# Induced attention and a leaky feed-forward in one program: attention products in common TensorE clusters, longer assumed landings

## The chip, the cores and the metric

The program runs on one core of a Trainium2 chip. Its engines are TensorE (matrix products into the eight PSUM banks), VectorE (DVE in the rows), ScalarE (ACT), GpSimd (POOL) and SyncE (SP), which issues the DMA transfers. Each engine takes its instructions in the order in which the program has them, and waits for semaphores of the others. The metric is device time in microseconds (us): 1604.66 us median of three runs before the change (1601.34 to 1604.69).

## The reference

```
def mab(q, kv):                       # one attention, 32 keys or queries "inducing"
    s = scale * (q @ kv.T);  s = s - s.max(-1)
    a = exp(s);  a /= a.sum(-1) + 1e-09
    return a @ kv
h   = mab(inducing, x)                # per batch: 32 x 128, over 12480 rows
y   = mab(x, h)                       # per batch: 12480 x 128
out = leaky(y @ w_in) @ w_out         # 49920 rows, 128 -> 2048 -> 128, slope 0.01
```

All is float32: `x` is 4 x 12480 x 128, `inducing` 32 x 128, `w_in` 128 x 2048, `w_out` 2048 x 128.

## The kernel before

*Algebra.* The second attention's weights for a row are 32 numbers, so `y @ w_in` is these weights times `h @ w_in`, a 32-row matrix per batch. Leaky ReLU is split into a ReLU part and a linear part; the linear part needs only `h @ (w_in @ w_out)`. Each float32 product is made of three products of rounded parts (high x high, high x low, low x high), which run in the faster float32r form; tiles called `hi` and `lo` are those parts.

*Tiles.* A batch has six groups of 2048 rows and one of 192 (number `RG` in the code). A group is four tiles of 512 columns; the 192-row groups of two batches share one tile, the pair tile, whose place is `PAIR_AT`. For each tile there are 16 blocks of the feed-forward width. A block has three first products (`A4` with `hwhi`, `hwlo`), a ReLU, a split into `ghi` and `glo`, and then second products with `w_hi` and `w_lo`, three in each of four row groups. All these products are row-tiled: 32 rows of the array each, four at once (`quarter`, line 988). The split of a block has two forms: near (ScalarE makes `ghi` from the bank, line 975, VectorE makes `glo`, line 978) and far (ScalarE copies the ReLU to `g`, GpSimd makes both parts, lines 1216 and 1218).

*Attention work.* Per batch and group there is a score product of the first attention (line 372, with `indT`), a small product that spreads the maxima (406), a value product (`xr` rows with the weights, 535), and later a score product of the second attention (372, with `hT`). At the end of a batch come a sum (605), a transposition of h (624), and the expansion of h through the weights (752, 768). These use the array in other tilings than line 988. The second attention's softmax goes through VectorE, GpSimd and ScalarE into a tile `aT`; `stack` (line 842 on) casts it into `both` (high part on ScalarE at line 856, low part on GpSimd at 863), and SyncE copies it (878) into the row-tiled form `A4`, of which there are three buffers. `both` has one buffer, `xr` nine.

*What sets the order.* From the third tile to the last but one a planner in the kernel, run when the program is built, writes out the order. It keeps a clock for each engine, assumes a time for each operation (`RELU`, `LOW`, `QUARTER` and so on) and for a transfer's landing (`LANDED`), and takes what can start soonest. Attention work stands in lanes (generators): stacking, stores, seconds (second scores), values, middles (maxima), scores. A lane that needs TensorE asks for it with the time from which it could run. `clustered` decides when such asks are served between the row-tiled products: when one has waited 9 us (`OLD`), when two stand there and one has waited 3 us (`PAIRED`), or when TensorE would be idle for 0.3 us (`IDLE`); up to three at once (`TOGETHER`). First products run up to ten blocks (`GB`) ahead of the second ones. `relu` takes the far form only where GpSimd would be done before the block's turn comes:

```
far = max(clock[POOL], start + RELU) + backlog(POOL) + FAR_HIGH + FAR_LOW
wanted = now[0] + (i - turn_of[0]) * SLOT - EARLY
if far_open[0] < 2 and left <= start and far <= wanted:
```

The first scores of batch b + 1 begin with the first tile of batch b (`begin`); values of a batch follow group by group (`first_values`), where the loads of the next group's `xr` are asked behind the value product.

Of the kernel before, what the change touches and what calls it, by code (L numbers as in the profile page):

```python
# [19 lines left out]
def induced_attention_then_leaky_ffn(  # L20
# [66 lines left out]
    XR = 9  # L87
# [6 lines left out]
    LANDED = 2300.0  # L94
# [360 lines left out]
    def first_scores(b):  # L455
# [15 lines left out]
        for g in [RG, *range(RG)]:  # L471
            _, J, K = GROUPS[g]
            w = 32 * K
            if g == RG:
# [30 lines left out]
            at = on_array("c", 875.0 if g != RG else 120.0, at, taken[0])  # L505
            if quads[0]:
# [14 lines left out]
    middles = []  # L521
# [48 lines left out]
    def first_values(b):  # L570
# [11 lines left out]
        for g in [RG, *range(RG)]:  # L582
# [7 lines left out]
            hp, at = multiplied(b, g, ay, at)  # L590
            yield from new(DVE, at)
# [3 lines left out]
            if g == RG - 1:  # L595
                yield from new(PE)
# [3 lines left out]

    def sums(b):

        pz = aux_ps("z_ps")
        same = e128.rearrange("p j m -> p (j m)")
        nc.tensor.matmul(pz[:, :1], same, sums_of.pop(b), start=True, stop=True)
        at = on_array("f", 64.0, taken[0])
        rz = sb.tile([P, 1], F32, tag="rz", name="rz")
        nc.vector.tensor_scalar_add(rz, pz[:, :1], 1e-9)
        nc.vector.reciprocal(rz, rz)
        done(pz, spent(DVE, 330.0, at))  # L610
        return rz

    def normalise(b, hacc, rz):
# [17 lines left out]
        hw[b] = [hT, None, None, False]  # L631
        landed[b, "h"] = at
# [109 lines left out]
    def expand_weights(b):  # L742

        hT = hw[b][0]
        hi = sb.tile([P, TOK + P], F32R, tag="hwhi", name="hwhi", bufs=2)
        lo = sb.tile([P, TOK + P], F32R, tag="hwlo", name="hwlo", bufs=2)
        if b:
            yield from new(PE, landed.get((b, "h"), 0.0))
# [7 lines left out]
        at = on_array("c", 875.0, landed.get((b, "h"), 0.0), taken[0])  # L756
# [4 lines left out]
        yield from old(HEAVY)  # L761

    def expand_linear(b):
        hT, hi, lo, _ = hw[b]
        if b:
            yield from new(PE, landed.get((b, "h"), 0.0))
        pw = aux_ps("m2_ps")
        nc.tensor.matmul(pw[:, :P], hT, w12, start=True, stop=True)
        at = on_array("f", 220.0, landed.get((b, "h"), 0.0), taken[0])
# [4 lines left out]
        yield from old()  # L774


    def second(b, g, eng=None):
        eng = eng or nc.gpsimd
        yield from until(lambda: g == RG or sum(q != RG for _, q in aT) < 4)
# [9 lines left out]
        del xT[b, g]  # L789
        ring.discard((b, g))  # L790
# [51 lines left out]
    def stack(tiles_, eng=None):  # L842
# [26 lines left out]
        for t, parts in tiles_:  # L869
            yield from until(lambda: len(A4) < A4_BUFS)  # L870
            a4 = sb.tile([P, 2, TOK], F32R, tag="A4", name="A4", bufs=A4_BUFS)
            to = 0
            for b, g, js in parts:
                w, o = 32 * GROUPS[g][2], at[b, g]
                for j in js:
                    yield from new(SP, when)
                    for r in range(4):
# [4 lines left out]
                        landed["A", t] = landed["both"] = spent(SP, 640.0, when) + LANDED  # L882
# [6 lines left out]
    def quick(t):  # L889
# [13 lines left out]
        if not qys:  # L903
            qys.append(sb.tile([P, QUICK, 4, M], F32, tag="both", name="qy", bufs=1))
# [34 lines left out]
    PAIR_AT = 4  # L939
# [145 lines left out]
    def after_h(b):  # L1085
        yield from first_values(b)
        yield from expand_weights(b)
        yield from expand_linear(b)
# [13 lines left out]
    with tc.manual_schedule():  # L1102
# [25 lines left out]
        seconds = [second(0, 0, nc.vector)] + [second(0, g) for g in [1, 2, RG, 3, 4, 5]]  # L1128
# [383 lines left out]
```

## Time and profile before

| | |
|---|---|
| three runs | 1601.34, 1604.66, 1604.69 us |
| profiled execution | 1606.44 us, span of the core's instructions 1604.7 us |
| mean granted TensorE clock | 0.986 |
| instructions | 60005 |

The profile comes from one execution. A row of the timeline has the start in us from the span's start, the duration, the engine, the line of the kernel, the operation, its tiles (out<-in) and how many were merged into the row; in brackets the idle time before it and who ended it. PE is TensorE, PEld its weight loads, SPq and ACTq are an engine's queue. The windows view with one line counts the instructions of that line that start in a stretch. The chain of waits is followed back from the last instruction, at each step to what released it. In the orders no time stands; they list the instructions of an engine as the program has them.

### The profile page before, as it was taken

The page shows a single profiled execution, that of the slowest core. Times are in us where ns is not written, and L with a number is a line of the kernel's source. Part 1 is how long each engine was busy: PE and PEld are TensorE (multiplying, and loading weights), DVE is VectorE, ACT ScalarE, POOL GpSimd, SP SyncE. Part 2 cuts the span into 40 slices and gives each one's busy share as a digit, 9 for nine tenths or more (in the row PEclk, how much of TensorE's full clock was granted, in tenths as well). Part 3 has the DMA queues.
Part 4 walks back from the last instruction along what each step waited for, and adds up shares of the span by engine and source line. Part 5 has one row for each costly group of instructions (what it writes and reads, how often), then busy time and mean ns, then how long its engine had stood idle before and what let it go on. Part 6 is the DMA issues. An engine that isn't in the chain of part 4 may idle for free.

```text
span 1604.7 us, 60005 instructions
## 1 busy us (share of the span) xinstructions
PE 1565.6 (98%) x25047; PEld 1360.7 (85%) x25047; DVE 1084.6 (68%) x1914; ACT 1080.4 (67%) x1957; POOL 1179.3 (73%) x1227
## 2 busy tenths in 40 slices
PE   7989999999999999999999999999999999999998
PEld 5658878899997876889999877789898899999996
DVE  6667886665666867666666876566666677666665
ACT  6446657777775655667777566677777777777774
POOL 2028716999998255699999458999999957778773
PEclk9899999999999999999999999999999999999999
DMA  7155653223254557323234667233233233232231
GB/s 266 16 115 98 126 140 74 50 56 62 35 109 70 101 103 151 82 55 61 48 62 93 109 125 159 60 64 58 46 70 58 37 67 63 55 65 53 57 61 21
DMA packets 400704, 128.49 MB, mean 80 GB/s; under 512 B 373136, under 2 KB 375600, under 8 KB 400432
## 3 DMA queue, kind: packets, MB, share of 16 engines
q1 hardware_dynamic: 399328, 124.50, 38.7%
q8 instruction: 197, 3.23, 0.8%
q14 instruction: 75, 0.61, 0.1%
q10 hardware_dynamic: 1104, 0.15, 0.1%
HBM read 48.94 MB, written 25.56 MB: 46 GB/s over the span
## 4 chain that ended last, share of the span: by engine, by line
PE 89%; SPq 4%; DMA 4%; DVE 2%; issue 1%; ACT 1%; POOL 0%; ACTq 0%; DVEq 0%; POOLq 0%
PE bank L988 83%; PE bank L372 2%; DMA xr<-in_x_dram 2%; SPq L878 2%; SPq L357 1%; PE bank L1018 1%; PE bank L535 1%; DVE glo L978 1%; DMA raw<-in_moe_w_in_dram 1%; SPq L346 0%; DMA A<-both 0%; POOL glo L1218 0%; ACT ghi L975 0%; PE bank L406 0%; DMA out_dram<-osb 0%
## 5 line engine op out<-in xcount | busy, mean ns | idle before, releaser
L988 PE MATMUL bank<-ghi,w_hi 32*128 32x512 f32 (+1 forms) x6080 | 1221.3, 393 | 4.8 <-ACT ghi L975 4.8
L988 PE MATMUL bank<-ghi,w_lo 32*128 32x512 f32 (+1 forms) x6080 | 1214.6, 392 | 0.0
L988 PE MATMUL bank<-glo,w_hi 32*128 32x512 f32 (+1 forms) x6080 | 1213.7, 392 | 0.0
L988 PE MATMUL bank<-A,hwhi 32*128 32x512 f32 (+1 forms) x3394 | 1051.6, 392 | 9.1 <-ACT g L975 3.6
L978 DVE SCALAR_TENSOR_TENSOR glo<-bank,ghi 128x512 fp32r<-128x512 f32 (+1 forms) x1052 | 697.3, 682 | 362.9 <-ACT ghi L975 345.3
L988 PEld LDWEIGHTS bank<-ghi,w_hi 32*128 32x128 f32 x6080 | 775.4, 184 | 42.9 <-ACT ghi L975 6.0
L988 PEld LDWEIGHTS bank<-glo,w_hi 32*128 32x128 f32 x6080 | 770.0, 184 | 35.2 <-issue 9.8
L988 PEld LDWEIGHTS bank<-ghi,w_lo 32*128 32x128 f32 x6080 | 773.4, 184 | 31.0 <-issue 5.8
L975 ACT ACTIVATE ghi<-bank 128x512 fp32r<-128x512 f32 (+1 forms) x1052 | 611.5, 598 | 217.4 <-PE bank L988 187.6
L1218 POOL TENSOR_TENSOR glo<-g,ghi 128x512 fp32r<-128x512 f32 (+1 forms) x516 | 668.1, 1295 | 41.3
L988 PE MATMUL bank<-A,hwlo 32*128 32x512 f32 (+1 forms) x1697 | 621.6, 390 | 0.0
L988 PEld LDWEIGHTS bank<-A,hwhi 32*128 32x128 f32 x3394 | 569.1, 184 | 38.1 <-DVE glo L978 7.3
L975 ACT ACTIVATE g<-bank 128x512 f32<-128x512 f32 (+1 forms) x516 | 308.6, 598 | 210.2 <-PE bank L988 174.3
L1216 POOL CAST ghi<-g 128x512 fp32r<-128x512 f32 (+1 forms) x516 | 316.4, 613 | 135.6 <-ACT g L975 96.0
L988 PEld LDWEIGHTS bank<-A,hwlo 32*128 32x128 f32 x1697 | 302.5, 184 | 6.2 <-issue 1.4
L1261 POOL TENSOR_TENSOR part<-part 128x512 f32<-128x512 f32 (+1 forms) x95 | 123.0, 1295 | 96.3 <-DVE part L1250 93.3
L1250 DVE TENSOR_TENSOR part<-bank,part 128x512 f32<-128x512 f32 (+1 forms) x190 | 129.8, 685 | 64.2 <-PE bank L988 42.8
L1244 ACT COPY part<-bank 128x512 f32<-128x512 f32 (+1 forms) x190 | 110.4, 583 | 18.1 <-PE bank L988 14.9
L1037 DVE STREAM_TRANSPOSE osb<-part 128x512 f32<-128x512 f32 (+1 forms) x95 | 66.6, 701 | 11.2 <-POOL part L1261 10.5
L826 POOL TENSOR_TENSOR y<-y,sm 128x512 f32<-128x512 f32 (+1 forms) x27 | 25.4, 941 | 32.0 <-DVE sm L822 17.2
L495 DVE STREAM_TRANSPOSE xT<-xc 128x512 f32<-128x512 f32 x72 | 47.4, 689 | 1.3 <-DMA xc<-in_x_dram 1.3
L863 POOL TENSOR_TENSOR both<-aT,both 128x512 fp32r<-128x512 f32 x24 | 31.1, 1296 | 20.9 <-DMA xr<-in_x_dram 12.5
(120 smaller groups left out, 632.5 us busy)
## 6 DMA issues: line engine op xcount, KB each, us to landing
A<-both SPq DMA_DIRECT2D x376, 128.0 KB, 2.4
xr<-in_x_dram SPq DMA_DIRECT2D x96, 256.0 KB, 4.6
out_dram<-osb SPq DMA_DIRECT2D x382, 64.0 KB, 2.2
xc<-in_x_dram SPq DMA_DIRECT2D x288, 64.0 KB, 2.9
raw<-in_moe_w_in_dram SPq DMA_DIRECT2D x4, 512.0 KB, 6.6
raw<-in_moe_w_out_dram SPq DMA_DIRECT2D x4, 512.0 KB, 6.8
A<-both SPq DMA_DIRECT2D x48, 16.0 KB, 1.8
out_dram<-osb SPq DMA_DIRECT2D x48, 8.0 KB, 1.8
```

Source lines behind the costliest of these rows:

```text
L372: nc.tensor.matmul(dst, lhsT, rhs, start=True, stop=True)
L495: nc.vector.transpose(t[:, j, :], blk.rearrange("p n c -> p (n c)"))
L878: nc.sync.dma_start(a4[32 * r : 32 * r + 32, :, to : to + w].bitcast(F32), both[32 * j : 32 * j + 32, :, o : o + w].bitcast(F32),)
L975: nc.scalar.activation(ghi[:, :n], ph[:, :n], AF.Relu)
L978: nc.vector.scalar_tensor_tensor(out=glo[:, :n], in0=ph[:, :n], scalar=0.0, in1=ghi[:, :n].bitcast(F32), op0=ALU.max, op1=ALU.subtract,)
L988: nc.tensor.matmul(dst, w[32 * r : 32 * r + 32], x[32 * r : 32 * r + 32], start=start, stop=stop, tile_position=(32 * r, 0),)
L1037: nc.vector.transpose(osb[:, :n], total[:, :n])
L1216: nc.gpsimd.tensor_copy(ghi[:, :n], g[:, :n])
L1218: nc.gpsimd.tensor_tensor(out=glo[:, :n], in0=g[:, :n], in1=ghi[:, :n].bitcast(F32), op=ALU.subtract)
L1244: nc.scalar.copy(part[:, :n], po[:, :n])
L1250: nc.vector.tensor_tensor(out=part[:, :n], in0=po[:, :n], in1=part[:, :n], op=ALU.add)
L1261: nc.gpsimd.tensor_tensor(out=total[:, :n], in0=total[:, :n], in1=part[:, :n], op=ALU.add)
```

## The change

The assumed landing of a transfer rises from 2300 to 3800 ns, with 3000 more for `xr` rows. `both` gets two buffers and `xr` seven in place of nine; `A4` is given back after its last use in the linear part, not at the tile's end. The first scores of batches 2 and 3 begin as soon as the weights of the batch before them are known, in place of its first tile, and follow at least 31 us a group (`PACE`); batch 1 begins as before and has the pace too. The sum of a batch is made in the last value product's cluster and in its bank. The two expansions of h stand in one cluster. `clustered` now waits for different times, by lane (`patience`): first scores 3 us, second scores 60 us or 3 us if their tile is no more than three tiles off, values and maxima 60 us while the batch's first scores go on; when one is over its time, all that are ready are served one behind the other (`gang`), with no row-tiled product between, and a bank may be held back for them. The pair tile moves from place 4 to 12 of its batch.

```diff
-    XR = 9
+    XR = 7
...
-    LANDED = 2300.0
+    LANDED = 3800.0
...
-    OLD, PAIRED, IDLE, HURRY, TOGETHER = 9000.0, 3000.0, 300.0, 9000.0, 3
+    IDLE, HURRY, APART, TAIL, WAITING, SOON = 300.0, 3000.0, 60000.0, 5000.0, 3000.0, 3000.0
+    NEAR, BANKS = 3, 1
+    PACE, STOCK = 31000.0, 4
...
-        landed[b, g, q] = spent(SP, 490.0) + LANDED
+        landed[b, g, q] = spent(SP, 490.0) + LANDED + 3000.0
...
-        for g in [RG, *range(RG)]:
+        began = now[0]
+        for n, g in enumerate([RG, *range(RG)]):
             _, J, K = GROUPS[g]
             w = 32 * K
+            yield from until(lambda: not quads[0] or now[0] >= began + n * PACE)
...
             hp, at = multiplied(b, g, ay, at)
+            if g == RG - 1:
+                if quads[0]:
+                    at, pz = totals(b, hp[:, 2 * C : 2 * C + 1])
+                else:
+                    pz = None
             yield from new(DVE, at)
+            if g == RG - 1 and pz is not None:
+                rz = inverse(pz, at)
...
+    def expand_both(b):
+        yield from until(lambda: b < 2 or max(t for t, p in enumerate(tiles) if any(q[0] == b - 2 for q in p)) < doing[0])
+        yield from new(PE, landed[b, "h"])
+        first = weights_product(b)
+        if not free:
+            yield from new(PE, landed[b, "h"])
+        second_ = linear_product(b)
+        yield from split_weights(b, *first)
+        yield from split_linear(b, *second_)
...
-        when = max(landed.get("both", 0.0), *(landed.get((b, g, "aT"), 0.0) for b, g in at))
+        when = max(landed.get(("both", 1), 0.0), *(landed.get((b, g, "aT"), 0.0) for b, g in at))
         yield from new(ACT, when)
-        both = sb.tile([P, 2, TOK], F32R, tag="both", name="both", bufs=1)
+        landed["both", 1] = landed.get(("both", 0), 0.0)
+        both = sb.tile([P, 2, TOK], F32R, tag="both", name="both", bufs=2)
...
-    PAIR_AT = 4
+    PAIR_AT = 12
...
+                    for g in [0, 1, 2, RG, 3, 4, 5]:
+                        seconds.append(second(b, g))
+                        coming.append((b, g))
+                    if b + 1 < B and quads[0]:
+                        scoring.append(b + 1)
+                        scores.append(first_scores(b + 1))
+                        values.append(after_h(b + 1))
...
-            if r == 3:
-                del A4[t]
...
                 if min(turn_of) > i:
                     del live[t, f]
+                    if f == LINEAR:
+                        del A4[t]
+                        landed["A4"] = at
...
-                spare = sorted(free)[wanting():]
+                spare = sorted(free)[wanting() + gathering[0] :]
...
         def patience(k):
-            if lanes[k] is seconds:
-                return HURRY if sum(g != RG for _, g in aT) < 2 else OLD
-            return OLD
+            lane = lanes[k]
+            if lane is scores:
+                return SOON
+            if lane is seconds:
+                b, g = coming[0]
+                here = work[min(firsts[0], len(work) - 1)][0]
+                if tile_of[b, g] - here <= NEAR or scores and len(ring) >= RING:
+                    return HURRY
+                return APART
+            return APART if lane and scoring and scoring[0] == finishing[0] else TAIL
...
+            if start < math.inf and all(ages[k] < patience(k) for k in ready) and start <= min(rows) + IDLE:
+                return False
+            there = sum(at <= start for at, _ in free)
+            if there < min(len(ready), BANKS) and start < math.inf and max(ages.values()) < WAITING + min(
+                patience(k) for k in ready
+            ):
+                gathering[0] = min(len(ready), BANKS)
+                if start <= min(rows) + IDLE:
+                    return False
+            gang.extend(sorted(ready, key=lambda k: (lanes[k] is middles or lanes[k] is values, -ages[k])))
+            return True
```

In the order of TensorE before, at the end of batch 1's values (`xr` and `ay`), the sum (`zs`) stands by itself in another bank:

```order
L988 MATMUL bank_66<-ghi,w_hi 128x512
L535 MATMUL bank_71<-xr,ay 32x128 x16
L988 MATMUL bank_64<-ghi,w_hi 128x512
L988 MATMUL bank_68<-A_3953,hwlo 128x512
L988 MATMUL bank_69<-ghi,w_hi 128x512
L988 MATMUL bank_66<-ghi,w_lo 128x512
L605 MATMUL bank_65<-zs,e_74 128x1
L988 MATMUL bank_64<-ghi,w_lo 128x512
```

In the changed order of TensorE the same place reads:

```order
L1028 MATMUL bank_66<-ghi,w_lo 128x512
L1028 MATMUL bank_68<-glo,w_hi 128x512
L541 MATMUL bank_67<-xr,ay 32x128 x16
L615 MATMUL bank_67<-zs,e_74 128x1
L1028 MATMUL bank_71<-A_5704,hwhi 128x512
L1028 MATMUL bank_69<-A_5704,hwhi 128x512
```

The sum has moved behind the value product, into the same cluster and bank. Elsewhere in the same way maxima (line 408 now) and values (541) of the first attention join its scores (374), or the second attention's.

On GpSimd, where the second scores of the last batch go through (`y` with `mx`), the order before has far blocks (`ghi`, `glo` from `g`) at nearly every row:

```order
L804 TENSOR_TENSOR y_26219<-y_26219,mx_26252 128x512
L1216 CAST ghi_26605<-g_26630 128x512
L1218 TENSOR_TENSOR glo_26606<-g_26630,ghi_26605 128x512
L1216 CAST ghi_26666<-g_26696 128x512
L1218 TENSOR_TENSOR glo_26667<-g_26696,ghi_26666 128x512
L1216 CAST ghi_26704<-g_26742 128x512
```

In the changed order of GpSimd, at the last batch's second scores, one tile's sum (`part`) follows the other:

```order
L842 TENSOR_TENSOR y_25974<-y_25974,mx_26124 128x512
L864 TENSOR_TENSOR y_25974<-y_25974,sm_26204 128x512
L1313 TENSOR_TENSOR part_26221<-part_26221,part_26266 128x512
L1313 TENSOR_TENSOR part_26551<-part_26551,part_26596 128x512
L1313 TENSOR_TENSOR part_26872<-part_26872,part_26928 128x512
L902 TENSOR_TENSOR both_27230<-aT_23122,both_27230 128x512
L1313 TENSOR_TENSOR part_27198<-part_27198,part_27270 128x512
```

Between two sums there is no far block: all 16 blocks of each of these tiles have moved to the near form, on ScalarE and VectorE.

## Rows read from the trace of the kernel before

**Rows 1.** The page, engine shares: busy us (share of the span) x instructions.

```profile
PE 1565.6 (98%) x25047; PEld 1360.7 (85%) x25047; DVE 1084.6 (68%) x1914; ACT 1080.4 (67%) x1957; POOL 1179.3 (73%) x1227
```

**Rows 2.** Windows of line 988: us, busy us (x starts), clock, DMA share, GB/s.

```profile
100.00:115.00 15.00, 7.69 (x73) 5.75 (x73) 0.77 0.78 183
505.00:520.00 15.00, 12.64 (x209) 10.24 (x208) 1.00 0.21 35
561.00:576.00 15.00, 11.37 (x148) 9.01 (x146) 0.77 0.26 50
628.00:642.00 14.00, 8.11 (x104) 6.33 (x108) 0.78 0.83 187
948.00:966.00 18.00, 12.49 (x192) 10.44 (x188) 0.91 0.80 148
195.00:250.00 55.00, 48.44 (x737) 40.62 (x731) 1.00 0.59 138
905.00:945.00 40.00, 36.62 (x524) 31.18 (x519) 1.00 0.63 111
1075.00:1100.00 25.00, 25.00 (x435) 23.96 (x431) 1.00 0.24 44
```

**Rows 3.** Timeline of TensorE, three clusters: start us, us, engine, line, operation.

```profile
440.69 0.39 PE L988 MATMUL bank<-ghi,w_hi 32*128 32x512 f32 x1
441.02 1.06 PE L372 MATMUL bank<-xT,hT 128*32 128x512 f32 x8
442.01 0.49 PE L988 MATMUL bank<-glo,w_hi 32*128 32x512 f32 x1
442.35 0.40 PE L988 MATMUL bank<-ghi,w_hi 32*128 32x512 f32 x2
...
944.06 0.39 PE L988 MATMUL bank<-ghi,w_lo 32*128 32x512 f32 x1
944.38 1.08 PE L535 MATMUL bank<-xr,ay 128*32 128x128 f32 x32
945.28 1.04 PE L372 MATMUL bank<-xT,indT 128*32 128x512 f32 x8
946.25 0.50 PE L988 MATMUL bank<-glo,w_hi 32*128 32x512 f32 x1
...
658.58 0.39 PE L988 MATMUL bank<-ghi,w_hi 32*128 32x512 f32 x2
659.21 0.49 PE L988 MATMUL bank<-glo,w_hi 32*128 32x512 f32 x1
```

**Rows 4.** Timeline of ScalarE, two places; in brackets the idle time before.

```profile
107.13 0.62 ACT L856 CAST both<-aT 128x512 fp32r<-128x512 f32 x1 [9.55 <-DMA out_dram<-osb]
...
567.79 0.62 ACT L856 CAST both<-aT 128x512 fp32r<-128x512 f32 x1 [4.42 <-DMA out_dram<-osb]
```

**Rows 5.** Timeline of TensorE at the second of them.

```profile
568.96 0.79 PE L988 MATMUL bank<-A,hwhi 32*128 32x512 f32 x1 [3.39 <-ACT g L975]
```

**Rows 6.** The chain that ended last, near 635 us: start us, us, what.

```profile
632.72 4.54 DMA xr<-in_x_dram
...
637.30 0.66 PE bank L535 x8
```

**Rows 7.** The page, DMA issues: KB each, median us to landing.

```profile
A<-both SPq DMA_DIRECT2D x376, 128.0 KB, 2.4
xr<-in_x_dram SPq DMA_DIRECT2D x96, 256.0 KB, 4.6
```

**Rows 8.** The page, groups of instructions: busy us, mean ns | idle before.

```profile
L978 DVE SCALAR_TENSOR_TENSOR glo<-bank,ghi 128x512 fp32r<-128x512 f32 (+1 forms) x1052 | 697.3, 682 | 362.9 <-ACT ghi L975 345.3
...
L1218 POOL TENSOR_TENSOR glo<-g,ghi 128x512 fp32r<-128x512 f32 (+1 forms) x516 | 668.1, 1295 | 41.3
...
L1037 DVE STREAM_TRANSPOSE osb<-part 128x512 f32<-128x512 f32 (+1 forms) x95 | 66.6, 701 | 11.2 <-POOL part L1261 10.5
```

**Rows 9.** Timeline of VectorE near 935 us.

```profile
935.70 2.48 DVE L978 SCALAR_TENSOR_TENSOR glo<-bank,ghi 128x512 fp32r<-128x512 f32 x4 [0.50 <-ACT ghi L975]
```

More of the change, by code (lines that the diff above doesn't have):

```diff
@@ L594, in first_values @@
             more(4 if g != RG else 1)
-            if g == RG - 1:
-                yield from new(PE)
+            if g == RG - 1 and pz is None:
                 rz = sums(b)
@@ L599, in first_values, with totals, inverse @@
         yield from normalise(b, hacc, rz)
+    def totals(b, pz):
+        same = e128.rearrange("p j m -> p (j m)")
+        nc.tensor.matmul(pz, same, sums_of.pop(b), start=True, stop=True)
+        return on_array("f", 64.0, landed.get((b, RG - 1, "e"), 0.0)), pz
+    def inverse(pz, at=0.0):
+        rz = sb.tile([P, 1], F32, tag="rz", name="rz")
+        nc.vector.tensor_scalar_add(rz, pz, 1e-9)
+        nc.vector.reciprocal(rz, rz)
+        spent(DVE, 330.0, at)
+        return rz
     def sums(b):
         pz = aux_ps("z_ps")
[L604 to L610, printed above, removed]
+        totals(b, pz[:, :1])
+        rz = inverse(pz[:, :1])
+        done(pz)
         return rz
@@ L740, in split, with weights_product @@
         return at
-    def expand_weights(b):
+    def weights_product(b):
         hT = hw[b][0]
[L745 to L748, printed above, removed]
         pw = aux_ps("hw_ps")
@@ L760, in expand_weights, with split_linear @@
         landed[b, "hw"] = at
[L761 to L769, printed above, removed]
+    def split_linear(b, pw, at):
+        _, hi, lo, _ = hw[b]
         at = yield from split(hi[:, TOK:], lo[:, TOK:], pw[:, :P], 1.0, P, at)
@@ L1387, in resume @@
                 got = (None, now[0])
-            asks[k] = got or (None, now[0] + 300.0)
+            asks[k] = got = got or (None, now[0] + 300.0)
+            asked[k] = max(now[0], got[1])
         def best(engine):
@@ L1416, in clustered @@
-            if (
-                start == math.inf
-                or any(ages[k] > patience(k) for k in ready)
-                or len(ready) > 1 and max(ages.values()) > PAIRED
-                or start > min(rows) + IDLE
-            ):
-                for k in sorted(ready, key=ages.get, reverse=True)[:TOGETHER]:
-                    if free:
-                        now[0] = max(now[0], max(rows))
-                        resume(k)
-                return True
-            return False
+            ready = gathered(start)
@@ new lines, in clustered @@
+            gathering[0] = 0
+            if not ready or not free:
+                return False
+            ages = {k: start - asked[k] for k in ready}
+            if start < math.inf and all(ages[k] < patience(k) for k in ready) and start <= min(rows) + IDLE:
[3 more added lines that the diff above has]
+                patience(k) for k in ready
+            ):
+                gathering[0] = min(len(ready), BANKS)
+                if start <= min(rows) + IDLE:
+                    return False
@@ L1441, in turn_over @@
                     choices.append((max(clock[SP], at + SIGNAL), 3, ("lane", k)))
-            options = [(*option(r), r) for r in range(4)] if quads_too else []
+            options = [(*option(r), r) for r in range(4)] if quads_too and not gang else []
             pe = min(options, key=lambda o: o[0], default=(math.inf, None, 0))
-            if pe[0] < math.inf or not choices:
+            if gang and free:
+                choices.append((max(*rows, now[0], min(free)[0]), 0, ("gang", 0)))
+            elif not gang and (pe[0] < math.inf or not choices):
                 choices.append((pe[0], 0, ("pe", pe)))
```

55 lines of the change are left out of this document (40 added, 15 removed).

## The prediction

> **What bounds the kernel now.** I read the page's engine shares first. TensorE is busy 1565.6 of 1604.7 us [rows 1], and no other engine passes 73 per cent, so only what TensorE does or waits for counts. But a busy share says little here, since four row-tiled products overlap in the array. So I went to the windows of line 988 alone, the row-tiled products of the feed-forward part. Undisturbed, 435 of them start in 25 us [rows 2], which is 57.5 ns each and 0.23 us for a round of four. There are 23,331 of them before and after the change, so this part (some 1340 us) cannot move. What can move is the rest: the attention products put between them, and stretches that fall short of 57.5 ns.
>
> The other windows of [rows 2] show the shortfall. From 100 to 115 us 73 products start where 261 fit, 10.8 us lost; 505 to 520: 209 of 261, 3.0; 561 to 576: 148 of 261, 6.5; 628 to 642: 104 of 243, 8.0; 948 to 966: 192 of 313, 7.0. In these stand one score product and a short value product, a short value product, a maximum, a value product with a maximum, and the same again. A full attention product costs 1.2 us with its cluster's ends and a maximum 0.5 (659.21 less 658.58, less the round of 0.23, and 0.11 as below) [rows 3], so I take off 1.6, 0.5, 0.5, 1.5 and 1.5. That leaves 9.2 + 2.5 + 6.0 + 6.5 + 5.5 = 29.7 us of stalls.
>
> Their causes stand in the timeline and the chain. At 107.13 and again at 567.79 ScalarE ran its cast into `both` after an idle wait of 9.55 and 4.42 us for transfers [rows 4]; the ReLUs stood behind it in the same queue, and TensorE came back at 568.96 after 3.39 us [rows 5]. At 637.30 TensorE began a value product after the 4.54 us landing of its `xr` rows [rows 6]. Four of the five windows have a granted clock of 0.77 to 0.91 [rows 2], so part of them ran at the lower of the two levels, 1.2 GHz, after the idle time; that is inside the 29.7.
>
> A second kind of loss has no single wait: from 195 to 250 us 737 start where 957 fit, and from 905 to 945 us 524 where 696 fit. That is 12.6 and 9.9 us. Six full products and three maxima stand in the first (8.7 us at these prices), three full ones, a short one and two maxima in the second (5.1); 3.9 and 4.8 us remain. There the first products run fewer than five blocks ahead of the second ones, so TensorE catches up with ScalarE and VectorE.
>
> **The change, part by part.**
>
> *Fewer clusters.* Over the orders, groups of attention products between row-tiled ones fall from 81 to 65 after the first 150 row-tiled products; the products themselves stay. A lone score product takes 440.69 to 442.01, less the round of 0.23 is 1.09, and the round behind it takes 0.34 for 0.23, so 1.20. A value and a score product together take 944.06 to 946.25, so 1.96, with the same end 2.07 [rows 3]. Two alone would be 2.40: joining saves 0.33. Sixteen times that is 5.3 us. The least it can save is the entry alone, 0.10 (0.33 from 440.69 to 441.02, less 0.23): 1.6. I take 4.5, near the measured pair.
>
> A rule speaks against this term. The Trainium skill, "TensorEngine Tiling (Array Packing)", Key Properties, says that changing the tiling mode drains the engine, whatever the number of clusters. The sum of maxima sits in another mode between score and value products, so by the orders mode changes fall only from 165 to 147. By that rule the term is 18 x 0.10 = 1.9 us in place of 4.5; the rows show the 0.10 at the entry.
>
> *`both` doubled, longer landings, loads asked earlier.* A cast into `both` now needs the transfers of the stack before last. In the order before, 64 to 185 row-tiled products (4 to 11 us) often lie between the last transfer out of `both` and the next cast; after, at least 450 (26 us). The planner counts 3.8 us for a landing and 6.8 for `xr`, where the page has medians of 2.4 and 4.6 [rows 7]. At the stalls of 628 and 948 us the value product stood 103 and 122 row-tiled products (6 and 7 us) behind its load; after, 157 (9 us) is the least and all others have 190 or more. `A4` is given back at its last use; its use stands 345 products or more behind its load except at the start, as before. So the stalls at 561, 628 and 948 should go, and the one at 505 most likely. At the start the first `A4` tile still has to land and the pipe to fill: I leave 3 of the 9.2 us, and 15 per cent of the other 20.5. Gain 6.2 + 17.3 = 23.5; bounds 12 (half of it turns up elsewhere) and 32 (all, and the small ones at 484 and 991 too).
>
> *Pacing and order.* Scores of batches 2 and 3 begin when the previous batch's weights are known and are spread at 31 us a group. Their work is unchanged. But ScalarE's two kinds of block shift: the orders give GpSimd 372 of 1568 blocks where the trace has 516 [rows 8]. 144 more go to VectorE, 144 x 0.682 = 98 us, which makes 1183 of some 1585 us, 75 per cent. The planner hands a block to GpSimd only when the first products are well ahead, so this tells of thin lead: counted in hundreds of row-tiled products, with the start and the end left out, the lead falls under 4.5 blocks in 34 hundreds, where it was 20. The two thin stretches above cost 8.7 us over 12.6 hundreds, 0.69 each; 14 more make 10 us at most, and nothing if VectorE is faster than planned. I take a loss of 6.
>
> *Banks in clusters.* A cluster of three or four products takes as many banks at once. For 9 of them (4 before, the last stage left out) the order has the bank's last reader within 14 products ahead. Each waits for one VectorE instruction at most, 0.68 us [rows 8]: 0 to 3.4 for the five more, taken as 2.5.
>
> *At nothing:* `xr` with 7 buffers instead of 9 (the next four loads are asked behind the value product either way, so the wait for its buffer is over; without that cover 4 loads would come up to 1 us later per group); the sum behind the last value product; the pair tile at place 12; hidden by weights known over 1500 row-tiled products ahead.
>
> **Sum.** -4.5 - 23.5 + 6 + 2.5 = -19.5. The profiled execution took 1606.4 us (1.7 outside its span), so 1586.9 for one like it; it lies 1.8 over the median of 1604.66, so 1585 for the median.
>
> **Rivals.**
>
> *A, all stalls go and the thin lead is free:* -5.3 - 32 = 1567. For it: four VectorE blocks in a row took 2.48 us [rows 9], so their starts lie 0.60 apart ((2.48 - 0.68) / 3) where the planner counts 0.69. Against it: the two thin stretches did cost 9 us with the same VectorE.
>
> *B, no change:* landings are long because the DMA engines are busy (share 0.83 and 0.80 in 628 to 642 and 948 to 966 [rows 2]), and other waits take their place. The stall term falls to its low bound and the thin lead rises to its high one: -4.5 - 12 + 10 + 3.4 = -3, 1602. Against it: the pacing takes the same loads out of the crowd.
>
> *C, slower, VectorE becomes the bound:* the order shows a stretch of 17 tiles, mostly in the last batch, in which GpSimd takes no block. There VectorE has 16 x 0.682 and three instructions of some 0.70, 13.0 us a tile [rows 8], against 244 x 57.5 ns = 14.0 us of TensorE. The four blocks of [rows 9] stood behind a wait of 0.50 us for ScalarE. If a block waits 0.2 us on the mean, a tile takes 16.2 us, 2.2 too long, 37 us in 17 tiles: 1604.7 - 19.5 + 37 = 1622. It decides from 19.5 / 17 = 1.15 us a tile on, which is a wait of 0.13 us a block. Against it: with starts 0.60 apart a tile needs 11.7 us, and a wait that falls into the 2.3 us left costs nothing.
>
> **How the numbers follow.** Forecast 0.63, A 0.18, B 0.10, C 0.09. What a measurement can tell from no change is 0.2 per cent, 3 us. The forecast and A are faster; B falls mostly within that bound (its 1602 lies just there), in small part a little under it; C is slower: faster 0.83, same 0.08, slower 0.09. The range goes from A (1567) to just past B (1603) and leaves out C and half of A's far side. The forecast's own range is 1574 to 1596.
>
> **What would show it.** Right: the cast into `both` no longer waits for a transfer; value products wait for `xr` under 2 us in total (7.0 is the sum of idle time before); the window around 100 to 115 us has some 180 row-tiled products; the clock stays at its upper level behind 115 us; lone scores are rarer. Wrong: VectorE busy over 90 per cent around the last batch's start with TensorE waiting on `glo` there (C); new waits of TensorE on `ghi` or `glo` of more than 20 us over the span (B); or stalls of over 3 us that recur with the clusters, from banks.

## The result and the profile after

The changed kernel takes 1583.6 us (median of 4 runs, 1583.19 to 1584.1); the kernel before, timed beside it, 1603.45 (1601.34 to 1604.69). The ratio is 0.9878 [0.9861, 0.9895], 1.2 per cent faster. The profiled executions took 1583.88 and 1606.44 us: 22.6 us to account for. The forecast was 1585.

The page of the changed kernel, engine shares (compare [rows 1]), then its groups for the blocks' low parts and the two kinds of transfer (compare [rows 7, 8]):

```profile
PE 1557.0 (98%) x25047; PEld 1367.8 (86%) x25047; DVE 1163.3 (74%) x2058; ACT 1077.5 (68%) x1957; POOL 913.6 (58%) x939
...
L1018 DVE SCALAR_TENSOR_TENSOR glo<-bank,ghi 128x512 fp32r<-128x512 f32 (+1 forms) x1196 | 787.5, 682 | 277.8 <-ACT ghi L1015 259.7
...
L1270 POOL TENSOR_TENSOR glo<-g,ghi 128x512 fp32r<-128x512 f32 x372 | 482.8, 1298 | 29.8
...
A<-both SPq DMA_DIRECT2D x376, 128.0 KB, 2.4
xr<-in_x_dram SPq DMA_DIRECT2D x96, 256.0 KB, 4.7
```

Read: the 144 blocks did move from GpSimd to VectorE (1052 to 1196 and 516 to 372) at unchanged prices, and the medians of the landings are what they were. What changed is when things wait. The windows of line 1028, which was 988 (compare [rows 2]; the granted clock is the third number from the right):

```profile
100.00:115.00 15.00, 9.24 (x112) 8.19 (x115) 0.89 0.80 186
195.00:250.00 55.00, 49.64 (x831) 42.27 (x829) 1.00 0.64 127
505.00:520.00 15.00, 14.07 (x235) 12.69 (x231) 1.00 0.63 121
561.00:576.00 15.00, 14.16 (x240) 11.92 (x232) 1.00 0.36 83
628.00:642.00 14.00, 12.76 (x219) 11.85 (x215) 1.00 0.19 32
905.00:945.00 40.00, 37.62 (x610) 34.72 (x606) 1.00 0.28 55
948.00:966.00 18.00, 18.00 (x309) 17.05 (x313) 1.00 0.21 41
1075.00:1100.00 25.00, 25.00 (x435) 24.94 (x431) 1.00 0.31 58
```

The stalls of 561, 628 and 948 us are gone, and outside the start no window falls below the upper clock level. (The same microseconds hold other work than before, so a window shows that a stall is absent, not the gain.) The start is half mended: 112 products where 73 were, 39 x 57.5 ns = 2.2 us. (The windows view counts the products that run in a stretch, so those begun just before it are in; the counts are up to 8 over the starts, in both kernels alike.) ScalarE there, in the timeline of the changed kernel (compare [rows 4, 5]):

```profile
105.31 0.62 ACT L895 CAST both<-aT 128x512 fp32r<-128x512 f32 x1 [6.41 <-DVE aT L875]
```

TensorE:

```profile
106.48 0.49 PE L1028 MATMUL bank<-ghi,w_hi 32*128 32x512 f32 x1 [3.12 <-DMA A<-both]
```

And the chain of waits behind it (compare [rows 6]):

```profile
97.59 0.66 SPq L348
...
101.43 0.60 SPq L918
...
102.08 4.38 DMA A<-both
...
106.48 0.73 PE bank L1028 x2
```

The cast now waits for its own data, `aT`, and no longer for a transfer. But TensorE waits for the transfers of `A4`, which SyncE issued behind a row of `xr` loads (line 348) and which took 4.38 us to land, against a median of 2.4.

The waits view (engine, line, releaser: us in total, times, longest). Before, for casts into `both` and for value products:

```profile
ACT both L856 <- DMA out_dram<-osb: 14.0, 2, 9.6
ACT both L856 <- DMA A<-both: 12.5, 5, 5.0
...
PE bank L535 <- DMA xr<-in_x_dram: 7.0, 7, 2.4
```

After, ScalarE's only wait of a cast, TensorE's waits for low parts, and all waits of the value products:

```profile
ACT both L895 <- DVE aT L875: 7.6, 2, 6.4
...
PE bank L1028 <- DVE glo L1018: 2.4, 3, 1.4
...
PE bank L541 <- DVE glo L1018: 0.6, 2, 0.4
...
PE bank L541 <- DVE ay L573: 0.2, 1, 0.2
```

The casts' 26.5 us of waits for transfers are gone, and so are the products' 7.0 us for `xr`. An example of a joined cluster, timeline of TensorE after (compare [rows 3]):

```profile
408.16 1.06 PE L374 MATMUL bank<-xT,hT 128*32 128x512 f32 x8
409.04 1.04 PE L374 MATMUL bank<-xT,indT 128*32 128x512 f32 x8
410.01 0.39 PE L408 MATMUL bank<-rd,e 128*128 128x4 f32 x2
410.33 0.49 PE L1028 MATMUL bank<-ghi,w_hi 32*128 32x512 f32 x1
```

Two score products and a maximum take 2.17 us from first start to the next row-tiled start: 0.88, 0.97 and 0.32, one end for three.

**Where the 22.6 us are.** I took the row-tiled products of each trace in hundreds, in the order of their starts (the first and the last hundred or so left out). Time above 57.9 ns a product (in proportion less for the narrow products of the pair tiles) is a cluster's where an attention product starts in the gap. The rest is excess, sorted by the order's lead of first over second products: "thin" hundreds fall under 4.5 blocks at their lowest, "stalls" are other hundreds over 0.25 us, "small" the remainder. The first hundred, at the start (102.8 to 117.0 us before, 102.7 to 114.5 after), has a thin lead too, but holds the stall shown above, so it is counted with the stalls: 8.4 us before, 5.4 after. In us:

| | clusters | of it waits for `xr` | thin (hundreds) | stalls | small | sum |
|---|---|---|---|---|---|---|
| before | 101.1 | 7.0 | 11.5 (20) | 26.9 | 10.0 | 149.5 |
| after | 89.4 | 0 | 14.9 (34) | 11.7 | 11.4 | 127.4 |

So 20.8 us came from stalls (15.2 + 7.0 for `xr`, less 1.4 more of small excess), 4.7 from clusters, and thin lead cost 3.4 us more, over 14 more hundreds.

### The profile page after: what moved, and what is told of

Its sections match the earlier page's. It is cut to its first block, busy times and chain, and to the rows that moved or that the text cites. A ratio compares the mean times of both kernels' runs of the same rounds, so it can differ in the third digit from the quotient of the medians.

```text
span 1581.9 us, 59727 instructions
## 1 busy us (share of the span) xinstructions
PE 1557.0 (98%) x25047; PEld 1367.8 (86%) x25047; DVE 1163.3 (74%) x2058; ACT 1077.5 (68%) x1957; POOL 913.6 (58%) x939
## 4 chain that ended last, share of the span: by engine, by line
PE 94%; DVE 3%; DMA 1%; ACT 1%; issue 0%; SPq 0%; POOL 0%; DVEq 0%; ACTq 0%; POOLq 0%
PE bank L1028 86%; PE bank L374 3%; PE bank L1058 2%; PE bank L541 1%; DVE glo L1018 1%; DMA xr<-in_x_dram 0%; DMA A<-both 0%; PE bank L408 0%; ACT ghi L1015 0%; PE bank L689 0%; DVE cv_a L203 0%; POOL glo L1270 0%; DVE xT L499 0%; PE bank L768 0%; DVE ay L573 0%
## 5 line engine op out<-in xcount | busy, mean ns | idle before, releaser
L1028 PE MATMUL bank<-ghi,w_hi 32*128 32x512 f32 (+1 forms) x6080 | 1199.0, 392 | 3.5 <-DMA A<-both 3.1
L1028 PE MATMUL bank<-glo,w_hi 32*128 32x512 f32 (+1 forms) x6080 | 1195.4, 391 | 0.0
L1028 PE MATMUL bank<-ghi,w_lo 32*128 32x512 f32 (+1 forms) x6080 | 1194.6, 390 | 0.0
L1028 PE MATMUL bank<-A,hwhi 32*128 32x512 f32 (+1 forms) x3394 | 1038.4, 391 | 3.1 <-DVE glo L1018 2.4
L1018 DVE SCALAR_TENSOR_TENSOR glo<-bank,ghi 128x512 fp32r<-128x512 f32 (+1 forms) x1196 | 787.5, 682 | 277.8 <-ACT ghi L1015 259.7
L1015 ACT ACTIVATE ghi<-bank 128x512 fp32r<-128x512 f32 (+1 forms) x1196 | 693.2, 598 | 262.5 <-PE bank L1028 215.7
L1028 PEld LDWEIGHTS bank<-glo,w_hi 32*128 32x128 f32 x6080 | 762.6, 183 | 26.9 <-issue 4.5
L1270 POOL TENSOR_TENSOR glo<-g,ghi 128x512 fp32r<-128x512 f32 x372 | 482.8, 1298 | 29.8
L1015 ACT ACTIVATE g<-bank 128x512 f32<-128x512 f32 x372 | 223.1, 600 | 159.7 <-PE bank L1028 134.5
L1268 POOL CAST ghi<-g 128x512 fp32r<-128x512 f32 x372 | 228.7, 615 | 163.1 <-ACT g L1015 106.2
L1296 ACT COPY part<-bank 128x512 f32<-128x512 f32 (+1 forms) x190 | 110.9, 586 | 21.6 <-PE bank L1028 17.4
L1077 DVE STREAM_TRANSPOSE osb<-part 128x512 f32<-128x512 f32 (+1 forms) x95 | 66.7, 702 | 13.6 <-POOL part L1313 13.2
L842 POOL TENSOR_TENSOR y<-y,mx 128x512 f32<-128x512 f32 (+1 forms) x27 | 25.4, 942 | 53.1 <-DVE mx L838 53.0
```

What stands on the lines that cost most here:

```text
L1015: nc.scalar.activation(ghi[:, :n], ph[:, :n], AF.Relu)
L1018: nc.vector.scalar_tensor_tensor(out=glo[:, :n], in0=ph[:, :n], scalar=0.0, in1=ghi[:, :n].bitcast(F32), op0=ALU.max, op1=ALU.subtract,)
L1028: nc.tensor.matmul(dst, w[32 * r : 32 * r + 32], x[32 * r : 32 * r + 32], start=start, stop=stop, tile_position=(32 * r, 0),)
L1077: nc.vector.transpose(osb[:, :n], total[:, :n])
L1268: nc.gpsimd.tensor_copy(ghi[:, :n], g[:, :n])
L1270: nc.gpsimd.tensor_tensor(out=glo[:, :n], in0=g[:, :n], in1=ghi[:, :n].bitcast(F32), op=ALU.subtract)
```

## Experiments

Each was timed beside the kernel before; ratios are to that. Theory S is the prediction's: the transfer edits (`both` doubled, longer landings) bring most of the gain.

**1 to 3, the transfer edits put alone into the kernel before.** `e1_both2` doubles `both`, with 7 `xr`; `e2_land` has the longer landings; `e3_both2_land` has both.

```diff
e1: -    XR = 9
    +    XR = 7
    -  both = sb.tile(..., name="both", bufs=1)
    +  both = sb.tile(..., name="both", bufs=2)
e2: -    LANDED = 2300.0
    +    LANDED = 3800.0
    -  landed[b, g, q] = spent(SP, 490.0) + LANDED
    +  landed[b, g, q] = spent(SP, 490.0) + LANDED + 3000.0
e3: both
```

> The kernel before with one part of the change: two buffers for `both` (and seven for `xr`, to make room), nothing else. Theory S (the gain is stalls behind transfers): the casts into `both` at the stage's start, near 484 and near 565 us no longer wait, some 10 us; the value products still wait for `xr` (least distance to the load 84 row-tiled products by the order), so 1593 us, half the gain. Rival K (the gain is the joined clusters: 77 groups here, 78 before, 62 after): 1603, no change. Rival P (the gain is the early, paced scores): 1603.

> The kernel before with the other part: landings taken as 3800 ns, 6800 for `xr`, one buffer of `both`. Theory S: no value product waits over 0.5 us for `xr` (least distance 159 products by the order, 103 before), which gives some 10 us; the casts still wait for transfers (distances 0, 65, 106 as before); thin lead in 32 hundreds in place of 21, at 0 to 0.7 us each: 1593 to 1600. Rivals K (80 groups) and P: 1603.

> The kernel before with both transfer parts and neither joined clusters (80 groups) nor early or paced scores. Theory S: nearly all of the gain, 1587 us (after plus 4 for 18 more groups); no cast and no value product waits for a transfer over 1 us. Rival K: 1600 or more, since no cluster is joined. Rival P: 1600 or more, and the crowded stretches near 600 and 950 us still lose some 15 us in waits of other kinds.

Measured: 1600.93 us, 0.9975 [0.9959, 0.9992]; 1618.95, 1.0094 [1.0076, 1.0112]; 1610.98, 1.0041 [1.0027, 1.0055]. Alone the transfer edits gain 0.25 per cent at best; together they lose. S is out by 8, 19 and 24 us, and no rival had e2 slower than 1603. TensorE in the waits view of e1:

```profile
PE bank L535 <- DMA xr<-in_x_dram: 12.2, 14, 2.7
```

ScalarE's casts and TensorE's products in that of e2:

```profile
ACT both L856 <- DMA out_dram<-osb: 15.2, 4, 9.4
ACT both L856 <- DMA A<-both: 14.3, 3, 7.9
...
PE bank L535 <- DMA xr<-in_x_dram: 3.3, 3, 2.5
```

In e1 no cast waits for a transfer, but the products' waits for `xr` rise from 7.0 to 12.2 us. In e2 those fall to 3.3, yet one buffer makes the casts wait as before (29.5 us), and thin lead rises to 21.3 us (11.5 before). In e3 no cast waits for a transfer, but the products wait 6.4 us for `xr`, thin lead costs 20.9 us, and one new stop costs 8.0. The window of line 989 and the chain show it:

```profile
525.00:536.00 11.00, 9.04 (x88) 8.35 (x92) 0.50 0.74 152
```

```profile
523.14 1.79 DMA A<-both
...
525.07 1.05 PE bank L989 x10
```

The transfers of an `A4` tile come late, and TensorE goes on at the lower clock level (0.50). Without this stop e3 would be at some 1603 (1611.0 - 8.0, an estimate), still no gain. S falls as an account of which edit pays.

**4, the changed kernel with the old serving of clusters** (`clustered` and `patience` of before; all else as after).

```diff
-            gang.extend(sorted(ready, ...))
-            return True
+            if (start == math.inf or any(ages[k] > patience(k) for k in ready)
+                or len(ready) > 1 and max(ages.values()) > PAIRED or start > min(rows) + IDLE):
+                for k in sorted(ready, key=ages.get, reverse=True)[:TOGETHER]:
...
```

> The changed kernel with the old rule for when attention products are served (9 us, 3 us for two, up to three), all else of the change kept: 83 groups, 173 mode changes, against 62 and 147. Theory S: 21 groups more at 0.2 to 0.33 us, 4 to 7 us, so 1588 to 1591; the waits for transfers stay gone. Rival K: 1600, most of the gain lost. Rival P: 1588 like S.

Measured: 1599.57, 0.9971 [0.996, 0.9983], the number of the clusters' theory. The order has 83 groups where the change has 62, counted alike, and the clusters cost 94.8 us for 89.4: 0.26 for each of the 21 (the prediction had 0.33). That is 5.4 of some 15; most of the rest is thin lead (27.4 us in 48 hundreds for 14.9 in 34).

**5 and 10, without the early start and the pace, and without the pace alone.**

```diff
e5, e10: -    PACE, STOCK = 31000.0, 4
         +    PACE, STOCK = 0.0, 4
e5 also: -            if b == 0 and (g, js) == (0, [0]):
         +            if (g, js) == (0, [0]) and b + 1 < B:
         -                    if b + 1 < B and quads[0]:
         -                        scoring.append(b + 1)
...
```

> The changed kernel without the early and paced scores: those of batch b + 1 begin with batch b's first tile, as before, and follow without a pace; transfers and the new serving of clusters stay. By the order 75 groups (62 in the changed kernel), thin lead in 55 hundreds of row-tiled products (35), value products at least 111 products behind their load. Theory L (what the change gains is thin lead that did not grow: every thin hundred costs 0.6 us, every group 0.26 us): 13 x 0.26 + 20 x 0.6 = 15 more, 1599. Rival G (the serving of clusters brings the gain by itself, the pace nothing): 1587.

> The changed kernel with the scores of the next batch begun early, as it has them, but with no pace between groups. By the order 69 groups (62), thin lead in 46 hundreds (35), nearest value product 117 behind its load. Theory L: 7 x 0.26 + 11 x 0.7 = 9.5 more, 1593: the early start carries the larger part of the 28 us of the run without both. Rival P (the pace carries it): 1605 or more.

Measured: e5 1611.88, 1.0040 [1.0026, 1.0053], slower than before though the stalls stay away (13.3 us, 26.9 before); both expectations for it (1599 and 1587) missed. e10 1591.71, 0.9938 [0.9921, 0.9955], near Theory L's 1593. By the ratios the pace is worth 0.0060, 10 us, and the early start, with no pace in either kernel, 0.0102, 16 us. Starts of row-tiled products by the windows view, 200 us each, show where:

| | 100 | 300 | 500 | 700 | 900 | 1100 | 1300 |
|---|---|---|---|---|---|---|---|
| before | 2740 | 3286 | 2812 | 3292 | 2846 | 3389 | 3476 |
| after | 2966 | 3088 | 3039 | 3042 | 3236 | 3376 | 3468 |
| e5 | 2633 | 3368 | 2843 | 3379 | 2715 | 3347 | 3472 |
| e10 | 2645 | 3032 | 3157 | 3111 | 3247 | 3413 | 3471 |

Before and e5 alternate between crowded and free stretches; after, the attention lies evenly. In e10 only the first stretch, batch 1's, which has no early start, is as crowded as in e5. Over the row the changed kernel starts 22,215 products and the kernel before 21,841; 374 x 57.5 ns is 21.5 us. What a crowded stretch looks like, windows of e5, all engines (PE, PEld, DVE, ACT, POOL; two crowded ones and a free one):

```profile
500.00:560.00 60.00, 59.67 (x879) 48.84 (x875) 53.35 (x103) 36.31 (x68) 10.80 (x11) 1.00 0.54 97
560.00:620.00 60.00, 59.69 (x847) 46.36 (x846) 54.26 (x104) 33.94 (x66) 7.60 (x8) 1.00 0.63 122
1100.00:1160.00 60.00, 60.00 (x1002) 55.17 (x999) 39.11 (x61) 43.14 (x75) 57.93 (x60) 1.00 0.30 57
```

TensorE's waits of line 1028 in e5, over the whole span:

```profile
PE bank L1028 <- DVE glo L1018: 3.7, 5, 1.4
PE bank L1028 <- ACT ghi L1015: 3.1, 1, 3.1
```

VectorE is 90 per cent busy and GpSimd 13 to 18; in the free stretch 65 and 97. The planner gives GpSimd hardly any blocks while lead is thin, so VectorE has them all, on top of the attention's own work, just when it has no room. Thin lead costs 38.9 us in e5. Of the 6.8 us in the waits view 4.5 fall at 55 and 105 us, so it shows 2.3 of them, and PE stays busy 59.7 of 60: with four products overlapping, a late block slows the rounds and leaves hardly any gap. Only the count of starts tells.

**6 and 9, the changed kernel with short landings (both terms as before), and also with one `both` and nine `xr`.**

```diff
e6, e9: -    LANDED = 3800.0
        +    LANDED = 2300.0
        -  ... + LANDED + 3000.0
        +  ... + LANDED
e9 also: XR = 9, both and qy with bufs=1
```

> The changed kernel with the landings of before (2300 ns, nothing more for `xr`), all else of the change kept. By the order 64 groups, thin lead in 24 hundreds (35), the value product nearest to its load 94 row-tiled products behind it (157). Theory L: 11 thin hundreds fewer give 6.6, two groups more cost 0.5, two value products wait for `xr` some 3 us each: 1583.5, the same. Rival S (the prediction's: longer landings are worth some 10 us): 1592 or more, with over 5 us of waits for `xr`.

> The changed kernel without its transfer part: one buffer for `both`, nine for `xr`, landings of 2300 ns; pace and new serving of clusters stay. By the order 55 groups (62 in the changed kernel), thin lead in 24 hundreds (35), but casts into `both` at 0, 16 and 39 products behind the last transfer out of it (450) and the nearest value product 112 behind its load (157). Theory S (the doubled `both` takes away stalls): groups and lead give 8.4, casts and one value product wait 12 to 15 us, 1588, with ScalarE idle for transfers at the casts and TensorE behind it. Rival Q (with the scores paced the transfers are early in any case, the transfer part is worth nothing): 1575.

Measured: e6 1583.55, 0.9869 [0.9853, 0.9886], as after and as Theory L had it; e9 1587.59, 0.9913 [0.9896, 0.9929], as S had it (1588). So the longer landings are worth nothing here, and the whole transfer part 4 to 6 us. The cast at the start in e9's timeline:

```profile
106.50 0.62 ACT L895 CAST both<-aT 128x512 fp32r<-128x512 f32 x1 [8.75 <-DMA A<-both]
```

All of ScalarE's waits for transfers at casts, in the waits view of e9:

```profile
ACT both L895 <- DMA A<-both: 12.2, 6, 8.8
ACT both L895 <- DMA out_dram<-osb: 1.4, 1, 1.4
```

With one buffer and evenly spread attention the casts wait 13.6 us for transfers where they waited 26.5, and 8.8 of it is the start (9.6 before). Outside the start 4.8 us are left of 16.9: the rest of the change takes most of these waits away without the transfer part.

**7, a planner that counts VectorE and ScalarE as they run.** It lets the next operation of either start 70 ns before the end of the one ahead.

```diff
-        clock[engine] = max([clock[engine], now[0], *(a + SIGNAL for a in after)]) + ns
-        return clock[engine]
+        at = max([clock[engine], now[0], *(a + SIGNAL for a in after)]) + ns
+        clock[engine] = at - (70.0 if engine in (ACT, DVE) and ns > 300.0 else 0.0)
+        return at
```

> The changed kernel with one thing else: the planner lets ScalarE's and VectorE's next instruction start 70 ns before the one ahead of it ends, as their rows in a row do (VectorE's starts lie 0.60 us apart at 0.682 us each). By the order 53 groups (62), thin lead in 11 hundreds (35). Theory L: 9 x 0.26 + 24 x 0.6 = 17 less, 1567. Rival N (thin lead is only a sign; the time beside the products stays): 1581, by the groups alone.

Measured: 1572.04 (1570.62 to 1572.65), 0.9794 [0.9779, 0.9808]. It beats both kernels, the changed one by 11.6 us (13 by the ratios; the two were not timed beside each other), between Theory L's 1567 and N's 1581. Thin hundreds fall from 34 to 10 and their cost from 14.9 to 2.5 us, as the theory of the lead has it; the groups fall to 53 and the clusters to 87.6. By the table's accounting thin lead gives 12.4 us, clusters 1.8, and 3.8 are lost in stalls and small excess: 10.4, against 11.2 between the two profiled executions. So thin lead still cost the changed kernel time, and most of that cost is gone here.

**8, more blocks for GpSimd** (the margin at which the planner hands it one goes from 1200 ns to 0).

```diff
-    EARLY, PREFER, YIELDING, PATIENCE = 1200.0, 0.0, 200.0, 15000.0
+    EARLY, PREFER, YIELDING, PATIENCE = 0.0, 0.0, 200.0, 15000.0
```

> The changed kernel with one number changed: a block may go to GpSimd when GpSimd is done with it by its turn, and not 1200 ns earlier. By the order 615 far blocks (372), thin lead in 15 hundreds (35), 63 groups. Theory L, with VectorE as what keeps the lead thin: 20 x 0.6 = 12 less, 1572, VectorE under 68 per cent busy. Rival N: 1584. Rival F (blocks from GpSimd come late, since its spans are longer than planned at times): 1590, with waits of TensorE on GpSimd's `glo`.

Measured: 1612.18, 1.0046 [1.0031, 1.0061]; all three expectations missed, though the far blocks rose and VectorE fell to 63 per cent as the order had it. Thin hundreds fall to 13 and still cost 13.9 us, and stalls are back with 38.4 us. Of these 14.5 stand in one hundred, from 1396 to 1417 us; its stop, in the chain of waits of e8:

```profile
1396.94 0.69 DVE part L1302
...
1401.39 1.28 POOL both L902
...
1408.51 1.80 DMA A<-both
```

TensorE behind it, in the timeline, then VectorE and GpSimd ahead of it:

```profile
1409.05 1.82 PE L1028 MATMUL bank<-A,hwhi 32*128 32x192 f32 x3 [5.78 <-DMA A<-both]
...
1396.94 0.69 DVE L1302 TENSOR_TENSOR part<-bank,part 128x512 f32<-128x512 f32 x1 [4.16 <-PE bank L1028]
...
1398.86 1.05 POOL L864 TENSOR_TENSOR y<-y,sm 128x512 f32<-128x512 f32 x1 [3.26 <-DVE sm L860]
```

Here the second scores' last steps, two of them GpSimd's, and the ten transfers behind them ran while TensorE already stood at their tile. The page has GpSimd 84 per cent busy, and in its timeline of the 19 us before them blocks follow each other with one gap of 0.37 us. But these blocks held only the first of the steps, by at most 1.8 us (the maxima were ready at 1392.79, `y` began at 1394.55). Then GpSimd itself stood idle for 3.26 us: VectorE had the sum of a tile (`part`) ahead in its queue, and that waited 4.16 us for TensorE. So the trace does not show the blocks on GpSimd as what made this stack late. The other stalls outside the start are spread, at most 1.4 us a hundred. What makes e8 slow stays open.

**11 and 12, the kernel of 7 with short landings, and with `SOON` at 5 us.**

```diff
e11: e7 with LANDED = 2300.0 and no 3000 for xr
e12: e7 with SOON = 5000.0
```

> The kernel with the overlap of 70 ns in the planner and the landings of before in one. By the order 53 groups, thin lead in 10 hundreds (53 and 11 with the longer landings). Theory L, and landings that are worth nothing: 1572, the same as with the longer landings. Rival S (longer landings matter once the lead is good): 1578 or more, with waits for `xr` of over 4 us.

> The kernel with the overlap of 70 ns in the planner, and first scores that wait 5 us in place of 3 before a cluster must be opened for them. By the order 51 groups (53), thin lead in 9 hundreds (11). Theory L: 2 x 0.26 + 2 x 0.8 = 2 less, 1570. Rival N (groups alone count): 1571.5.

Measured: e11 1582.15, 0.9876 [0.9858, 0.9893]; e12 1572.61, 0.9812 [0.9788, 0.9835], the same as e7, so its two theories are not told apart. e11's 10 us do not come from `xr`, for which no value product waits. One stop stands out. SyncE's queue in the timeline of e11:

```profile
644.95 11.68 SPq L360 DMA_DIRECT2D xc<-in_x_dram  x16
656.80 4.35 SPq L919 DMA_DIRECT2D A<-both  x7
```

TensorE in the same timeline:

```profile
659.23 0.49 PE L1029 MATMUL bank<-A,hwhi 32*128 32x512 f32 x1 [1.79 <-DMA A<-both]
```

And the window of line 1029 around it:

```profile
655.00:668.00 13.00, 9.14 (x71) 6.84 (x63) 0.70 0.80 158
```

SyncE issued 16 loads of `xc` ahead of the transfers of a stack that was due; TensorE waited for these, and has 71 starts for 226 at a granted clock of 0.70: 8.9 us short, of which a cluster that begins at 666.39 takes 1.6 and a maximum 0.5. No expectation had this: L had 1572, and S its 1578 or more by waits for `xr`. So one late stack makes up most of the 10. That the short landings put the loads there was not tried apart, and stays open.

## Why the prediction was right, and where it was not

**The time** was right within 1.4 us, and the terms as read from the trace held: stalls behind transfers went, clusters were joined, thin lead grew. By the terms:

- *Clusters, 4.5*: 4.7 by the table. The rule of the Trainium skill that was weighed, "TensorEngine Tiling (Array Packing)", Key Properties, gave 1.9 with the entry alone. In e4 there are 21 more groups, 26 more mode changes (173 for 147) and 5.4 us more: 0.26 a group or 0.21 a change. Entry (0.10) and exit (0.11) [rows 3] are two changes, and every group has both, so a group has 0.21 by the rows. At 0.10 a change, as the prediction priced the rule, e4 would cost 2.6 us more: half of what it does. That price was too low; whether changes or groups are what counts, two differences can't tell.
- *Stalls, 23.5*: 20.8. The shortfall is the start: I gave it 6.2 and it brought 2.2 by the window, 3.0 by the hundreds. The step assumed that the cast's wait was all; with that gone, the `A4` transfers behind the `xr` loads in SyncE's queue were next. The window of 100 to 115 us has 112 products and not 180. The casts, the `xr` waits and the clock behind 115 us came as listed.
- *Thin lead, a loss of 6*: 3.4. The 14 more hundreds came (34, as foreseen), but a hundred costs 0.44 us on the mean where it cost 0.57. I had priced them at 0.69, from two crowded windows of the kernel before.
- *Banks, 2.5*: nothing of it to be seen; TensorE's longest wait for a VectorE result in lines 408 and 541 is 1.0 us.

Two readings of the prediction were off without much effect. Of the 435 products that the windows view counts from 1075 to 1100 us 427 start there, so one takes 58.5 ns and not 57.5; the losses by window change by 0.3 us at most, but for 505 to 520 us, where 25 products are narrow ones of the pair tile and 1 us more was lost. And 18 x 0.10 is 1.8, and 85 per cent of 20.5 is 17.4.

So the misses are 2.7, 2.6 and 2.5 us, the first against the other two; that 1585 came within 1.4 is in part luck. **The step that failed** is the attribution: "*`both` doubled, longer landings, loads asked earlier*" were said to bring 23.5 because the waits that end stand at transfers. The waits do, and the gain does not follow. Put alone into the kernel before, these edits make it between 0.25 per cent faster and 0.94 slower; taken out of the changed kernel they cost 4 to 6 us, the landings none. The serving in clusters is worth 15 and the pace 10, each taken out by itself, and the early start some 16, taken out where the pace was gone already. With the transfer part's 5 that adds up to 46, where all together bring 20. They are not additive. I put that down to the planner, which makes the whole order anew with each, and to one quantity on which all of them act, how far ScalarE and VectorE run ahead; no run takes this apart. Nor does any run take out the earlier return of `A4`, the joined expansions of h, the sum's new place or the pair tile's. I had listed the pacing as a change that leaves the work and costs lead. It does the opposite: it spreads VectorE's attention work, and with it the transfers that collided.

| | ratio | clusters | thin (hundreds) | stalls |
|---|---|---|---|---|
| e2 landings in before | 1.0094 | 105.9 | 21.3 (31) | 27.1 |
| e5 no early start, no pace | 1.0040 | 93.6 | 38.9 (54) | 13.3 |
| e4 old serving | 0.9971 | 94.8 | 27.4 (48) | 11.0 |
| e10 no pace | 0.9938 | 90.2 | 26.7 (45) | 9.8 |
| e9 no transfer part | 0.9913 | 89.3 | 10.2 (23) | 19.5 |
| after | 0.9878 | 89.4 | 14.9 (34) | 11.7 |
| e7 spacing | 0.9794 | 87.6 | 2.5 (10) | 13.1 |

The table, by the accounting above with the start among the stalls, shows how much each varies between these kernels: thin lead by 36 us, clusters by 18, stalls by 17.

**Rival C**, VectorE the bound, was to show in the stretch of the last batch, and did not. Window of all engines after (PE, PEld, DVE, ACT, POOL):

```profile
1150.00:1350.00 200.00, 200.00 (x3404) 190.19 (x3400) 173.10 (x271) 146.22 (x257) 38.86 (x37) 1.00 0.30 58
```

VectorE in the timeline there (compare [rows 9]):

```profile
1206.20 3.21 DVE L1018 SCALAR_TENSOR_TENSOR glo<-bank,ghi 128x512 fp32r<-128x512 f32 x5
```

VectorE is 87 per cent busy and TensorE keeps its rate: 3376 starts of line 1028 from 1100 to 1300 us, 3389 before. Five blocks in 3.21 us start 0.63 apart ((3.21 - 0.69) / 4), so the room that spoke against C was there. A VectorE without room did come where I had not looked for it, in the crowded stretches of e5. **Rival A** at 1567, no cost for thin lead, is nearly what e7 reached, by telling the planner of the spacing that spoke for A (0.62 for 0.69, where 0.60 is measured).

Open stay what makes e8 slow, e11's late stack, the growth of thin lead in e2 and e3 (the longer assumed landings shift when the planner issues everything else; no run takes that apart), and whether `SOON` matters.

## What to carry to other kernels

A wait that stands out in the trace is not yet the edit that pays: here the edits aimed at the waits gave 5 us and those that spread the work 10 to 16 each. Where TensorE runs several products at once, count starts per stretch against an undisturbed one, since here a thin lead showed neither as a wait nor as a lower busy share. When a planner sets the order, first bring its durations to the start-to-start times that the trace shows; one such number was worth over half as much as this whole change.

## What the hardware showed unexpectedly

- A stretch that loses 8 us of 60 to thin lead reads as busy throughout: e5 from 560 to 620 us has TensorE busy 59.69, with 743 row-tiled starts where 1043 fit (17.3 us short), and some 9 us of that are clusters.
- A transfer of 128 KB landed in a median of 2.4 us and took 4.38 behind `xr` loads, at a DMA share of 0.80.
- An idle time is followed by the lower clock level (a granted clock of 0.50), and work goes on at it: three windows of line 1028 in e8, ahead of the stop, from the stop on, and the 11 us behind it.

```profile
1398.00:1403.00 5.00, 1.63 (x13) 0.89 (x11) 1.00 0.15 26
1404.00:1417.00 13.00, 7.70 (x71) 7.22 (x75) 0.50 0.48 100
1409.00:1420.00 11.00, 10.70 (x148) 10.22 (x152) 0.63 0.63 125
```

The 148 products of the last are all narrow ones of the pair tile (76 of 384 columns, 72 of 192). At 57.5 ns for 512 columns they are 4.8 us of work: 6.2 of the 11 us are lost after the stop, to the lower clock and to transfers that still come in one by one.
